# Attention features and a gated FFN on one core: Strassen products from batch 2 on, six PSUM banks for attention, omega by another queue

## The chip, the cores and the metric

The kernel runs on one core of a Trainium2 chip. The metric is the device time of one execution in microseconds. The time before is the median of three runs; the profile comes from one further execution of the same program.

## The reference

Linear attention with positive random features, then a feed-forward block with a gate. Sizes: batch B = 8, heads H = 8, sequence S = 576, head dimension D = 64, 128 features, model width 512, inner width 2048.

```python
def phi(x):                                   # x = q or k, scaled by 1 / D**0.25
    proj = einsum('bhsd,md->bhsm', x, omega)
    sq = sum(x * x, axis=-1, keepdims=True) / 2
    h = proj - sq
    h = h - max(h, axis=-1, keepdims=True)
    return exp(h) / sqrt(m)
...
kv  = einsum('bhsm,bhsd->bhmd', k_p, v)
z   = sum(k_p, axis=2)
num = einsum('bhsm,bhmd->bhsd', q_p, kv)
den = einsum('bhsm,bhm->bhs', q_p, z)[..., None] + 1e-06
x = (num / den).transpose(0, 2, 1, 3).reshape(B * S, H * D)
...
h = x @ w_in
sp = log1p(exp(h))
out = (h * erf(sp)) @ w_out
```

## The kernel before, in words

**The two halves of the work.** Attention is done by pairs of heads, 32 pairs in all, four to a batch. The pairs of batch 0 go one by one (`first`, `project_pair`); all later ones go in *quads* of two pairs (`attention`, `project`), of which each pair holds the keys or queries of two heads. For a quad, `project` multiplies keys or queries by omega in three groups of six matmuls of 128x128. Each of them uses only half of the rows of TensorE's array (64 of 128): pair j of the quad lies in the rows of its half, and its factor is `wq` for j = 0 and `wk` for j = 1 (both hold omega, in opposite halves). Each group fills two PSUM banks, one per pair (tiles `ppk_...` for keys and `ppq_...` for queries), and is followed by a maximum on VectorE, a shift, and an exponential on ScalarE, after which the two banks are free. `key_values`, `turn` and `attend` follow: keys times values (`kvp`), the queries' features turned (`pt`), numerator and denominator (`nd`), division into `xs`. `split` turns `xs` into a rounded half `xh` and a remainder `xl`.

The feed-forward block takes one batch at a time, in two *phases* ph = 0, 1 of 1024 inner columns each. A phase has four *granules* fp of the first product (256 columns each) and four blocks et of the second product. `BLOCKS` interleaves the granules of one phase with the second products of the phase before it. The operands of every product are held as a rounded part and a remainder, so a product takes three matmuls of 128x288: high by high, remainder by high, high by remainder. The one exception is the last product of attention, `nd`, for the pairs below `WHOLE` (8): these use whole F32 operands, and so have no remainders `ql` and `kl`.

**The first product in blocks.** A granule is a 2x2 block product. In the batches below `PLAIN` (3) `plain1` does it with eight block products, 48 matmuls (tiles `h...`). From batch `PLAIN` on `gemm1` does it with seven (the table `PRODUCTS`), 42 matmuls: their operands are sums of weight blocks (`S1` to `S4`) and of x blocks (`T1` to `T4`), and eight outputs are drained from PSUM, seven of them with an addition on VectorE (`hadd`, rows `hs<-hS,hs`) where `plain1` drains four with a copy (`hout`).

**The weights.** A weight unit (128 x 512) is made once from the 64-bit numbers in which it comes (`make`): a load `st`, a scaling copy `wt` on POOL (GpSimd) or ScalarE, three integer instructions on VectorE in a PSUM buffer `pw`, a rounded copy and a remainder `w`. It is then stored to DRAM (`wdw`) and fetched again for every later batch (`w<-wdw`). `make_sums` makes the sums S1 to S4 in batch PLAIN - 1, from two units of each granule: the two units are put together again (`R`, two instructions), four differences and sums (`S`), then rounded part and remainder (`cS`) in two units, both stored. `R` takes its buffer from the stream of `wt` and `S` from that of `st`, each of two buffers (`CAPS`).

**What sets the order.** `Plan` records all operations with their reads and writes. `Plan.order` plays the program through with costs for each operation (`COST` and the numbers at each `pl.op`), due times that follow from `plan=` and from successors, pools with a number of buffers (`SLOTS`), and streams with a cap on how many buffers are in use at a time (`CAPS`; `att` is the number of PSUM banks that attention may hold, 5 of 8, beside `moe1`, `moe2` and `pw`). Of the operations that an engine could start it takes the one that is due first. Going from full to half rows on TensorE or back costs half of `COST["turnout"]`, and after a projection the planner looks for another projection that is ready within `NEAR`. The result is one list, and every engine runs its instructions in exactly that order (`InOrder`); SyncE issues nearly all transfers, also in that order. So a change of one number can move instructions anywhere.

All instructions are recorded by one helper, so they all have the same line in the profile (L842) and are told apart by tile names. `ph`, `fp`, `et`, batch and pair numbers are in the names; the profile's groups leave them out.

**The start.** Omega comes by two transfers of POOL's queue into `om`; VectorE scales it and copies it to `wk` and `wq`. The keys and queries of pair 0 come by SyncE's queue in three parts each.

Of the kernel before, what the change touches and what calls it, by code (L numbers as in the profile page):

```python
# [10 lines left out]
F32 = mybir.dt.float32  # L11
F32R = mybir.dt.float32r
I32 = mybir.dt.int32
AF = mybir.ActivationFunctionType
ALU = mybir.AluOpType
# [40 lines left out]
            ("S4", "B22", (((0, 1), (0, 1)),)))  # L56


COST = dict(mm=0.132, proj=0.224, turnout=0.33, tr=0.109, kv=0.222, table=1.3)
LAG = {"T": 0.35, "A": 0.35, "V": 0.33, "G": 0.33, "S": 0.3}  # L60
SLOTS = dict(w=8, u=2, un=2, f=2, mx=2, sq=2, v=2, qh=1, ql=1, kh=1, kl=1, rc=2, xs=4, xh=2, xl=2, u2=2,
             hs=4, gs=2, gh=6, gl=6, os=4, ps=8)
CAPS = dict(st=2, wt=2, cv=2, att=5, moe1=3, moe2=2)

# [253 lines left out]
AHEAD = 40.0  # L318

BLOCKS = (("f", 0), ("f", 1), ("e", 0), ("f", 2), ("e", 1), ("f", 3), ("e", 2), ("e", 3))  # L320
WHOLE = 8
PLAIN = 3
PAIR = 6.9
FIRST = 11.5
LEAD = 30.0
# [13 lines left out]
RESTS0 = 15.0  # L339
SQA = 4.0  # L340
NEAR = 6.0
WHG = 5.0
WBG = -1e9


def build(emit):
# [190 lines left out]
    def project(m, qk, t0):  # L537
        a = quads[m]
        u, sq = a["u" + qk], a["sq" + qk]
        for j, x in enumerate(a["pairs"]):  # L540
            x["f" + qk] = pl.tile("f", f"f{qk}{x['nm']}", [P, NC, P])
        mx = pl.tile("mx", f"mx{qk}{a['nm']}", [P, 2, NC])
        for i in range(3):
            pps = [pl.tile("ps", f"pp{qk}{x['nm']}_{i}", [P, 512], F32, "att")
                   for x in a["pairs"]]
            pl.op("proj" + qk, [("T", 3 * COST["proj"], -1e9)],
                  lambda e, i=i, pps=pps: E.project(pps, u, i),
                  reads=[(u, 0)], writes=[(pp, 0) for pp in pps] + [(x["f" + qk], "room") for x in a["pairs"]], plan=quad_time(m, t0 + 0.02 * i))
            for j, pp in enumerate(pps):
                pl.op("max" + qk, [("V", 0.47, -1e9)], lambda e, i=i, j=j, pp=pp: E.maximum(sq.ap[:, j, :, 2], pp, i),  # L550
                      reads=[(pp, 0)], writes=[(sq, (j, (2, i)))])
            pl.op("shift" + qk, [("V", 0.17, -1e9)], lambda e, i=i: E.shift(mx, sq, i),
                  reads=[(sq, (j, x)) for j in range(2) for x in (0, 1, (2, i))],
                  writes=[(mx, (i, j)) for j in range(2)])
            for j, (x, pp) in enumerate(zip(a["pairs"], pps)):
                f = x["f" + qk]
                pl.op("exp" + qk, [("A", 0.77, -1e9)],
                      lambda e, i=i, j=j, f=f, pp=pp: E.exponential(f, mx, pp, i, j),
                      reads=[(pp, 0), (mx, (i, j))], writes=[(f, i)], set="exp")

    def key_values(n, t0):
        a = pairs[n]
        f, v = a["fk"], a["v"]
        kvp = a["kvp"] = pl.tile("ps", "kvp" + a["nm"], [P, 512], F32, "att", early(n))
        for j in range(2):
            pl.op("kv", [("T", (5 - j) * COST["kv"], -1e9)], lambda e, j=j: E.key_values(kvp, f, v, j),
                  reads=[(f, i) for i in range(3)] + [(v, 0)], writes=[(kvp, 0)],
                  plan=when(n, t0 + 0.08 * j))
        whole = n < WHOLE
        kh = a["kh"] = pl.tile("kh", "kh" + a["nm"], [P, 2, P], F32 if whole else F32R)  # L570
        kl = a["kl"] = kh if whole else pl.tile("kl", "kl" + a["nm"], [P, 2, P], F32R)
        pl.op("kvhigh", [("V", 0.4, -1e9), ("A", 0.4, -1e9)], lambda e: E.kv_high(e, kh, kvp),
              reads=[(kvp, 0)], writes=[(kh, 0)])
        if not whole:
            pl.op("kvrest", [("V", 0.4, -1e9)], lambda e: E.kv_rest(kl, kvp, kh),
                  reads=[(kvp, 0), (kh, 0)], writes=[(kl, 0)])

    def turn(n, t0):
# [246 lines left out]
def tile_attention_moe(ctx: ExitStack, tc: tile.TileContext, qT, kT, qN, kN, vP, omT, w1, w2, out):  # L825
# [66 lines left out]
    class Emit:  # L892
# [92 lines left out]
        def project(self, pps, u, i):  # L985
            for c in range(3):
                for j, pp in enumerate(pps):
                    r = slice(j * D, (j + 1) * D)
                    pe.matmul(pp.ap[:, c * P:(c + 1) * P],
                              lhsT=u.ap[r, (3 * i + c) * P:(3 * i + c + 1) * P], rhs=(wk if j else wq)[r],  # L990
                              start=True, stop=True)

        def maximum(self, m, pp, i):
            dve.tensor_reduce(m[:, 3 * i:3 * i + 3],
                              pp.ap[:, :3 * P].rearrange("p (c m) -> p c m", c=3), axis=AX.X,
                              op=ALU.max, negate=True)

        def shift(self, mx, sq, i):
            dve.tensor_reduce(mx.ap[:, :, 3 * i:3 * i + 3], sq.ap[:, :, 3 * i:3 * i + 3], axis=AX.X, op=ALU.add)

        def exponential(self, f, mx, pp, i, j):
            m = mx.ap if j is None else mx.ap[:, j]
            for c in range(3):
                act.activation(f.ap[:, 3 * i + c, :], pp.ap[:, c * P:(c + 1) * P], AF.Exp,
                               bias=m[:, 3 * i + c:3 * i + c + 1])
# [177 lines left out]
```

## Time and profile before

| what | us |
|---|---|
| median of three runs (lowest, highest) | 1059.65 (1059.07, 1060.84) |
| profiled execution | 1060.85 |
| span of the profiled execution | 1058.4 |
| mean granted clock of TensorE | 0.998 |

The span runs from the first to the last instruction that the trace records; the profiled execution's own time is 2.45 us longer than its span. An engine's busy time is the sum of what its instructions took, or less where they overlap. In a row of groups the operation stands with its output, an arrow, its inputs, their shapes and the count; behind the bar its busy time, the mean of one in ns, and the idle time of the engine before such instructions with what ended most of it. The view of waits has a waiting group, what it waited for, and then the total in us, the count and the mean. The timeline has the start, the duration and the row. A window has, for each engine, its busy time and in brackets the number of instructions.

The start of each half batch can be read from the first instruction of its first product: batch 0 starts at 36.7 us and its second half at 92.1, batch 1 at 159.6 and 239.0, batch 2 at 305.6 and 372.1, batch 3 at 439.0 and 501.9. The last second product ends at about 1054.8.

### The profile page before, as it was taken

How to read it: one execution, taken by the hardware profiler on the slowest of the kernel's cores; microseconds unless marked ns; L12 is line 12 of the kernel's file. 1: busy time of each engine (PE TensorE's matmuls, PEld its weight loads, DVE VectorE, ACT ScalarE, POOL GpSimd, SP SyncE). 2: the span in 40 equal slices, each digit the busy share in tenths (PEclk: the TensorE clock that was granted, in tenths of full speed). 3: DMA queues.
4: the chain of work that ended last, by engine and by line, in shares of the span. 5: the costliest groups of instructions: out<-in, count | busy, mean ns of one | idle time of the engine just before them, and what ended most of it. 6: DMA issues, size and time to landing. Idle time of an engine off the chain costs nothing.

```text
span 1058.4 us, 21952 instructions
## 1 busy us (share of the span) xinstructions
PE 1042.0 (98%) x8272; PEld 1014.2 (96%) x8272; DVE 752.0 (71%) x1488; ACT 681.9 (64%) x1302; POOL 458.8 (43%) x458
## 2 busy tenths in 40 slices
PE   7999999999999999999999999999999999999998
PEld 7889989999999999999999999999999999999998
DVE  5999997885587586765878766686677756765551
ACT  7879977776577766866647666485666656453330
POOL 6637446434297584632345243452326211443300
PEclk9999999999999999999999999999999999999999
DMA  8675878686366686668767677677866756668761
GB/s 256 207 269 184 281 260 280 232 297 227 130 226 227 250 289 239 218 209 296 251 236 233 234 257 243 220 249 261 259 203 227 235 181 226 222 231 265 269 234 49
DMA packets 77736, 247.81 MB, mean 234 GB/s; under 512 B 8736, under 2 KB 9120, under 8 KB 77632
## 3 DMA queue, kind: packets, MB, share of 16 engines
q1 hardware_dynamic: 77568, 246.35, 68.9%
q8 instruction: 66, 1.08, 0.4%
q14 instruction: 38, 0.31, 0.1%
q0 software_dynamic: 64, 0.07, 0.0%
HBM read 211.78 MB, written 34.60 MB: 233 GB/s over the span
## 4 chain that ended last, share of the span: by engine, by line
PE 92%; DVE 3%; DMA 2%; POOL 1%; issue 1%; SPq 1%; ACT 0%; DVEq 0%; POOLq 0%; ACTq 0%
PE o L842 39%; PE h L842 14%; PE hS L842 12%; PE hA L842 9%; PE kvp L842 5%; PE nd L842 4%; PE ppq L842 3%; PE ppk L842 3%; PE pt L842 2%; DMA uq<-qT 1%; DVE pw L842 1%; SPq L842 1%; POOL unq L842 0%; POOL uq L842 0%; POOL unk L842 0%
## 5 line engine op out<-in xcount | busy, mean ns | idle before, releaser
L842 PE MATMUL o<-gh,w 128*128 128x288 f32 x2048 | 458.7, 301 | 2.8 <-DVE w L842 2.5
L842 PEld LDWEIGHTS o<-gh,w 128*128 128x128 f32 x2048 | 341.5, 188 | 11.4 <-DVE w L842 3.0
L842 PE MATMUL o<-gl,w 128*128 128x288 f32 x1024 | 301.7, 295 | 0.0
L842 PEld LDWEIGHTS o<-gl,w 128*128 128x128 f32 x1024 | 192.9, 188 | 0.2
L842 PE MATMUL h<-xh,w 128*128 128x288 f32 x768 | 173.9, 303 | 0.3 <-ACT xh L842 0.3
L842 POOL TENSOR_TENSOR hs<-gs,hs 128x576 f32<-128x576 f32 x64 | 96.5, 1532 | 163.3 <-ACT gs L842 132.6
L842 PE MATMUL hS<-xh,wS 128*128 128x288 f32 x640 | 156.3, 297 | 0.1
L842 PEld LDWEIGHTS h<-xh,w 128*128 128x128 f32 x768 | 129.6, 190 | 1.9 <-ACT xh L842 0.5
L842 POOL TENSOR_TENSOR gl<-hs,gh 128x576 fp32r<-128x576 f32 x60 | 100.0, 1690 | 61.2 <-ACT gh L842 30.9
L842 PE MATMUL hA<-xh,w 128*128 128x288 f32 x480 | 122.1, 298 | 0.4 <-DVE u L842 0.4
L842 ACT ACT_TABLE_LOAD x92 | 118.0, 1283 | 2.4 <-PEq L1174 0.7
L842 PE MATMUL h<-xl,w 128*128 128x288 f32 x384 | 114.1, 297 | 0.5 <-POOL xl L842 0.5
L842 POOL TENSOR_TENSOR unq<-unq 128x288 f32<-128x288 f32 (+2 forms) x62 | 47.0, 759 | 153.0 <-ACT unq L842 146.5
L842 PEld LDWEIGHTS hS<-xh,wS 128*128 128x128 f32 x640 | 112.1, 188 | 0.3 <-DVE u L842 0.3
L842 ACT ACTIVATE fk<-ppk,mxk 128x128 f32<-128x128 f32 x288 | 79.2, 386 | 39.2 <-DVE mxk L842 35.1
L842 PE MATMUL hS<-xl,wS 128*128 128x288 f32 x320 | 94.3, 295 | 0.0
L842 ACT ACTIVATE rc<-nd,eps 64x288 f32<-64x288 f32 x128 | 63.5, 496 | 42.3 <-PE nd L842 40.0
L842 ACT ACTIVATE fq<-ppq,mxq 128x128 f32<-128x128 f32 x288 | 78.9, 386 | 16.6 <-DVE mxq L842 12.5
L842 ACT ACTIVATE gs<-hs 128x1152 f32<-128x1152 f32 x64 | 72.9, 1163 | 22.3 <-DVE hs L842 21.9
L842 PEld LDWEIGHTS hA<-xh,w 128*128 128x128 f32 x480 | 85.6, 188 | 0.6 <-DVE u L842 0.6
L842 POOL TENSOR_TENSOR unk<-unk 128x288 f32<-128x288 f32 (+2 forms) x72 | 58.5, 816 | 55.0 <-ACT unk L842 27.3
L842 PEld LDWEIGHTS h<-xl,w 128*128 128x128 f32 x384 | 73.0, 190 | 1.1 <-POOL xl L842 0.7
(111 smaller groups left out, 2127.1 us busy)
## 6 DMA issues: line engine op xcount, KB each, us to landing
w<-wdw SPq DMA_DIRECT2D x184, 512.0 KB, 4.5
wS<-wdcS SPq DMA_DIRECT2D x80, 512.0 KB, 4.3
st<-w SPq DMA_DIRECT2D x32, 512.0 KB, 4.4
wdw<-w SPq DMA_DIRECT2D x32, 512.0 KB, 3.9
v<-vP SPq DMA_DIRECT2D x32, 325.0 KB, 4.1
w<-wdw SPq DMA_DIRECT2D x40, 256.0 KB, 3.9
out<-os SPq DMA_DIRECT2D x32, 288.0 KB, 4.0
wdcS<-cS SPq DMA_DIRECT2D x16, 512.0 KB, 5.1
```

The costliest lines, as they stand in the source:

```text
L842: return tc.keep_in_program_order(method(*args, **kwargs))
```

## The change

There are four edits.

1. `PLAIN` goes from 3 to 2: batch 2 uses seven block products in place of eight, and the weights' sums are made in batch 1 in place of batch 2. `WHOLE` goes from 8 to 12: the attention of batch 2 uses whole F32 operands in `nd`.
2. `R` and `S` get a stream of their own (`sr`, `ss`), one buffer each, out of the same pools.
3. Attention may hold six PSUM banks; the planner's cost of a change of rows goes from 0.33 to 0.40. `project` and what follows it are written for any division of the nine chunks into groups (`GROUPS`); the table given has the same three groups of three, and `f` is now tracked by chunk.
4. Omega comes by two transfers of SyncE's queue, ahead of the first keys, directly to `wk` and `wq`, and is scaled there by two instructions; `om` and the two copies are gone.

```diff
-COST = dict(mm=0.132, proj=0.224, turnout=0.33, tr=0.109, kv=0.222, table=1.3)
+COST = dict(mm=0.132, proj=0.224, turnout=0.40, tr=0.109, kv=0.222, table=1.3)
...
-CAPS = dict(st=2, wt=2, cv=2, att=5, moe1=3, moe2=2)
+CAPS = dict(st=2, wt=2, cv=2, att=6, moe1=3, moe2=2)
...
-WHOLE = 8
-PLAIN = 3
+WHOLE = 12
+PLAIN = 2
...
+GROUPS = ((0, 3), (3, 6), (6, 9))
...
-        r = pl.tile("gh", f"R{ph}_{fp}", [P, 2, 2, BW], F32, "wt")
+        r = pl.tile("gh", f"R{ph}_{fp}", [P, 2, 2, BW], F32, "sr", 1)
...
-        s = pl.tile("gl", f"S{ph}_{fp}", [P, 4, BW], F32, "st")
+        s = pl.tile("gl", f"S{ph}_{fp}", [P, 4, BW], F32, "ss", 1)
...
-    om = sb.tile([P, P], F32, name="om", tag="os0")
-    pool.dma_start(om[D:P], omT)
-    pool.dma_start(om[0:D], omT)
+    sp.dma_start(wk[D:P], omT)
+    sp.dma_start(wq[0:D], omT)
...
-    dve.tensor_scalar_mul(om, om, 1.0 / math.sqrt(math.sqrt(D)))
-    dve.tensor_copy(wk[D:P], om[D:P])
-    dve.tensor_copy(wq[0:D], om[0:D])
+    for w in (wk[D:P], wq[0:D]):
+        dve.tensor_scalar_mul(w, w, 1.0 / math.sqrt(math.sqrt(D)))
```

Three places show how the order moves. The first is **TensorE's** order at the keys' projections of the second quad of batch 5. `ppk_2` and `ppk_3` are the banks of its two pairs, `uk` its keys, `o` a second product with gates `gh`, `gl` and a weight unit `w`. The last number of a name is a running one. Before:

```order
L842 MATMUL ppk_2_0_7844<-wq,uk_7081 128x128
L842 MATMUL ppk_3_0_7845<-wk,uk_7081 128x128
L842 MATMUL ppk_2_0_7844<-wq,uk_7081 128x128
L842 MATMUL ppk_3_0_7845<-wk,uk_7081 128x128
L842 MATMUL ppk_2_0_7844<-wq,uk_7081 128x128
L842 MATMUL ppk_3_0_7845<-wk,uk_7081 128x128
L842 MATMUL o_1_1_1_7857<-gh_1_0_6931,w_1_1_0_151_7631 128x288
L842 MATMUL o_1_1_1_7857<-gl_1_0_6955,w_1_1_0_151_7631 128x288
L842 MATMUL o_1_1_1_7857<-gh_1_0_6931,w_1_1_0_151_7631 128x288
L842 MATMUL o_1_1_0_7785<-gh_1_1_6949,w_1_1_0_151_7631 128x288
```

After:

```order
L858 MATMUL ppk_3_0_7866<-wk,uk_7076 128x128
L858 MATMUL ppk_2_3_7877<-wq,uk_7076 128x128
L858 MATMUL ppk_3_3_7878<-wk,uk_7076 128x128
L858 MATMUL ppk_2_3_7877<-wq,uk_7076 128x128
L858 MATMUL ppk_3_3_7878<-wk,uk_7076 128x128
L858 MATMUL ppk_2_3_7877<-wq,uk_7076 128x128
L858 MATMUL ppk_3_3_7878<-wk,uk_7076 128x128
L858 MATMUL ppk_2_6_7886<-wq,uk_7076 128x128
L858 MATMUL ppk_3_6_7887<-wk,uk_7076 128x128
L858 MATMUL ppk_2_6_7886<-wq,uk_7076 128x128
L858 MATMUL ppk_3_6_7887<-wk,uk_7076 128x128
L858 MATMUL ppk_2_6_7886<-wq,uk_7076 128x128
```

Before, one group of six stands alone between pieces of the second product, and 27 matmuls of the second product follow before the next group. After the change the three groups of the quad stand next to each other.

The second place is **VectorE's** order in the second half of batch 0, where the unit `w_0_2_1` of the second weight is made (three numbers: half, block, part). `pw_0_2_1` is the PSUM buffer in which it is put together, `xl` a remainder of x, `sqk` and `mxk` belong to the maxima of a quad's keys. The last row shown is the last step of the unit. Before:

```order
L842 TENSOR_TENSOR w_0_2_0_21_1880<-pw_0_2_0_1993,w_0_2_0_21_1880 128x2x256
L842 TENSOR_REDUCE mxk_1944<-sqk_1522 128x2x3 x2
L842 TENSOR_SCALAR pw_0_2_1_2052<-wt_0_2_1_2018 128x512
L842 SCALAR_TENSOR_TENSOR pw_0_2_1_2052<-st_0_2_1_1963,pw_0_2_1_2052 128x512 x2
L842 TENSOR_TENSOR xl_0_2054<-xs_2_1806,xh_0_2035 128x576
L842 TENSOR_TENSOR xl_1_2072<-xs_3_1900,xh_1_2040 128x576
L842 TENSOR_TENSOR w_0_2_1_22_1964<-pw_0_2_1_2052,w_0_2_1_22_1964 128x2x256
```

After:

```order
L858 TENSOR_REDUCE mxk_2008<-sqk_1519 128x2x3 x2
L858 TENSOR_SCALAR pw_0_2_1_2024<-wt_0_2_1_1978 128x512
L858 SCALAR_TENSOR_TENSOR pw_0_2_1_2024<-st_0_2_1_1926,pw_0_2_1_2024 128x512
L858 TENSOR_REDUCE sqk_1519<-ppk_0_6_2014 128x3
L858 TENSOR_REDUCE sqk_1519<-ppk_1_6_2015 128x3
L858 TENSOR_REDUCE mxk_2008<-sqk_1519 128x2x3
L858 SCALAR_TENSOR_TENSOR pw_0_2_1_2024<-st_0_2_1_1926,pw_0_2_1_2024 128x512
L858 TENSOR_TENSOR xl_1_2066<-xs_1_1247,xh_1_2029 128x576
L858 CAST w_0_2_1_22_1927<-pw_0_2_1_2024 128x2x256
L858 TENSOR_TENSOR w_0_2_1_22_1927<-pw_0_2_1_2024,w_0_2_1_22_1927 128x2x256
```

The unit's last step is row 250 of VectorE before and row 246 after. TensorE's first matmul with this unit is row 691 of its own before and row 700 after.

The third place is **POOL's** order in the first half of batch 1. `unk` and `unq` are squares of keys and queries of a later batch, `wt_1_1_1` and `wt_1_1_0` the scaling copies of units of the second weight's second half, `R`, `S` and `cS` belong to the weights' sums, `hs` is a gate. Before:

```order
L842 TENSOR_TENSOR unk_0_2496<-unk_0_2496 128x576
L842 TENSOR_TENSOR unk_0_2496<-unk_0_2496 128x9x32
L842 TENSOR_TENSOR unk_0_2496<-unk_0_2496 128x9x16
L842 TENSOR_SCALAR unk_0_2496<-unk_0_2496 128x9x16
L842 TENSOR_TENSOR unk_1_2514<-unk_1_2514 128x576
L842 TENSOR_TENSOR unk_1_2514<-unk_1_2514 128x9x32
L842 TENSOR_TENSOR unk_1_2514<-unk_1_2514 128x9x16
L842 TENSOR_SCALAR unk_1_2514<-unk_1_2514 128x9x16
L842 TENSOR_SCALAR wt_1_1_1_2640<-st_1_1_1_2539 128x512
L842 TENSOR_TENSOR hs_0_0_2351<-gs_0_0_2557,hs_0_0_2351 128x576 x2
```

After:

```order
L858 TENSOR_TENSOR S_1_2455<-R_1_2384,S_1_2455 128x256
L858 TENSOR_TENSOR cS_1_0_2510<-S_1_2455,cS_1_0_2510 128x2x256
L858 TENSOR_SCALAR cS_1_1_2550<-S_1_2455 128x2x256
L858 TENSOR_TENSOR R_2_2561<-w_0_4_31_2386 128x512
L858 TENSOR_TENSOR R_2_2561<-w_0_5_32_2432 128x512
L858 TENSOR_SCALAR wt_1_1_0_2611<-st_1_1_0_2543 128x512
L858 TENSOR_TENSOR unq_2_2153<-unq_2_2153 128x9x32
L858 TENSOR_TENSOR unq_2_2153<-unq_2_2153 128x9x16
```

Before, the copy `wt_1_1_1` stands behind the folds of two keys' squares. After the change the copy `wt_1_1_0` stands behind instructions of the sums: the last difference of the second granule's `S`, its `cS`, and both `R` of the third granule, which read units fetched from DRAM. In both programs two of the eight copies of that half are on POOL (`wt_1_1_1` and `wt_1_3_0` before, `wt_1_1_0` and `wt_1_3_0` after); the others are on ScalarE.

More of the change, by code (lines that the diff above doesn't have):

```diff
@@ L508, in project_pair @@
                   plan=pair_time(n, t0 + 0.05 * i))
-            pl.op("max" + qk, [("V", 0.47, -1e9)], lambda e, i=i, pp=pp: E.maximum(mx.ap, pp, i),
+            pl.op("max" + qk, [("V", 0.47, -1e9)], lambda e, i=i, pp=pp: E.maximum(mx.ap[:, 3 * i:3 * i + 3], pp.ap[:, :3 * P]),
                   reads=[(pp, 0)], writes=[(mx, i)])
-            pl.op("exp" + qk, [("A", 0.77, -1e9)], lambda e, i=i, pp=pp: E.exponential(f, mx, pp, i, None),
-                  reads=[(pp, 0), (mx, i)], writes=[(f, i)], set="exp")
+            pl.op("exp" + qk, [("A", 0.77, -1e9)], lambda e, i=i, pp=pp: E.exponential(
+                [(f, 3 * i + c, mx.ap[:, 3 * i + c:3 * i + c + 1], pp, c) for c in range(3)]),
+                  reads=[(pp, 0), (mx, i)], writes=[(f, 3 * i + c) for c in range(3)], set="exp")
     def load(m, qk):
@@ L542, in project @@
         mx = pl.tile("mx", f"mx{qk}{a['nm']}", [P, 2, NC])
[L543 to L559, printed above, removed]
@@ new lines, in project @@
+        fs = [x["f" + qk] for x in a["pairs"]]
+        for i, (first_, end) in enumerate(GROUPS):
+            pps, parts, place = [], [], {}
+            for c in range(first_, end, 4):
+                w = min(4, end - c)
+                both = False
+                for j in range(1 if both else 2):
+                    pp = pl.tile("ps", f"pp{qk}{a['pairs'][j]['nm']}_{c}", [P, 512], F32, "att")
+                    pps.append(pp)
+                    js = (0, 1) if both else (j,)
+                    chunks = [(x, c + k) for x in js for k in range(w)]
+                    place.update({x: (pp, k) for k, x in enumerate(chunks)})
+                    parts.append((pp, js, c, w, chunks))
+            pl.op("proj" + qk, [("T", (end - first_) * COST["proj"], -1e9)],
+                  lambda e, place=place: E.project(place, u),
+                  reads=[(u, 0)], writes=[(pp, 0) for pp in pps] + [(f, "room") for f in fs],
+                  plan=quad_time(m, t0 + 0.02 * i))
+            for k, (pp, js, c, w, chunks) in enumerate(parts):
+                n = len(chunks)
+                pl.op("max" + qk, [("V", 0.07 + 0.133 * n, -1e9)],
+                      lambda e, pp=pp, js=js, c=c, w=w, n=n: E.maximum(
+                          sq.ap[:, js[0]:js[-1] + 1, c:c + w, 2], pp.ap[:, :n * P]),
+                      reads=[(pp, 0)], writes=[(sq, (2, i, k))])
+            pl.op("shift" + qk, [("V", 0.17, -1e9)], lambda e, a=first_, b=end: E.shift(mx, sq, a, b),
+                  reads=[(sq, (j, x)) for j in range(2) for x in (0, 1)]
+                  + [(sq, (2, i, k)) for k in range(len(parts))], writes=[(mx, i)])
+            for pp, _, _, _, chunks in parts:
+                pl.op("exp" + qk, [("A", 0.02 + 0.25 * len(chunks), -1e9)],
+                      lambda e, pp=pp, chunks=chunks, place=place: E.exponential(
+                          [(fs[j], c, mx.ap[:, j, c:c + 1], pp, place[j, c][1]) for j, c in chunks]),
+                      reads=[(pp, 0), (mx, i)], writes=[(fs[j], c) for j, c in chunks], set="exp")
@@ L566, in key_values @@
             pl.op("kv", [("T", (5 - j) * COST["kv"], -1e9)], lambda e, j=j: E.key_values(kvp, f, v, j),
-                  reads=[(f, i) for i in range(3)] + [(v, 0)], writes=[(kvp, 0)],
+                  reads=[(f, c) for c in range(NC)] + [(v, 0)], writes=[(kvp, 0)],
                   plan=when(n, t0 + 0.08 * j))
@@ L586, in turn @@
             pl.op("turn", [("T", 3 * COST["tr"], -1e9)], lambda e, i=i, pt=pt: E.turn(pt, a["fq"], i),
-                  reads=[(a["fq"], i)], writes=[(pt, 0)], plan=when(n, t0 + 0.05 * i))
+                  reads=[(a["fq"], 3 * i + c) for c in range(3)], writes=[(pt, 0)], plan=when(n, t0 + 0.05 * i))
             pl.op("turnhigh", [("A", 0.39, -1e9), ("V", 0.47, -1e9)],
@@ L983, in sum_squares, with project, maximum, shift @@
                               axis=AX.X, op=ALU.add, negate=bool(x))
[L985 to L1005, printed above, removed]
+        def project(self, place, u):
+            for (j, c), (pp, k) in sorted(place.items(), key=lambda x: (x[0][1], x[0][0])):
+                r = slice(j * D, (j + 1) * D)
+                pe.matmul(pp.ap[:, k * P:(k + 1) * P], lhsT=u.ap[r, c * P:(c + 1) * P],
+                          rhs=(wk if j else wq)[r], start=True, stop=True)
+        def maximum(self, m, src):
+            dve.tensor_reduce(m, src.rearrange("p (j c m) -> p j c m", m=P, j=m.shape[1]) if len(m.shape) > 2
+                              else src.rearrange("p (c m) -> p c m", m=P), axis=AX.X, op=ALU.max,
+                              negate=True)
+        def shift(self, mx, sq, a, b):
+            dve.tensor_reduce(mx.ap[:, :, a:b], sq.ap[:, :, a:b], axis=AX.X, op=ALU.add)
+        def exponential(self, parts):
+            for f, c, m, pp, k in parts:
+                act.activation(f.ap[:, c, :], pp.ap[:, k * P:(k + 1) * P], AF.Exp, bias=m)
         def key_values(self, kvp, f, v, j):
```

## The prediction

> **What bounds the kernel now.** I read the page first: the shares of busy time and the chain.
>
> ```profile
> span 1058.4 us, 21952 instructions
> PE 1042.0 (98%) x8272; PEld 1014.2 (96%) x8272; DVE 752.0 (71%) x1488; ACT 681.9 (64%) x1302; POOL 458.8 (43%) x458
> ...
> PE 92%; DVE 3%; DMA 2%; POOL 1%; issue 1%; SPq 1%; ACT 0%; DVEq 0%; POOLq 0%; ACTq 0%
> ```
>
> TensorE (PE) is busy in 98% of the span and makes 92% of the chain, so what PE no longer has to issue shortens the run. VectorE (DVE) has 71%, but an average hides a stage in which it is full, and a 98% share says nothing of how the remaining 16 us are spread, so next I asked for the stages. By the first product of each batch, 100:172 is the end of batch 0 and the start of batch 1, 172:237 and 237:302 are batch 1, 302:372 and 372:437 are batch 2, 437:500 is the first half of batch 3.
>
> ```profile
> 100.00:172.00 72.00, 69.36 (x560) 64.98 (x560) 66.18 (x127) 60.36 (x134) 37.35 (x44) 1.00 0.80 269
> 172.00:237.00 65.00, 65.00 (x528) 63.16 (x526) 54.57 (x106) 47.33 (x91) 27.91 (x27) 1.00 0.78 264
> 237.00:302.00 65.00, 65.00 (x521) 63.57 (x520) 37.48 (x74) 43.94 (x84) 29.01 (x28) 1.00 0.53 179
> 302.00:372.00 70.00, 70.00 (x567) 68.02 (x566) 49.61 (x87) 48.88 (x95) 51.58 (x49) 1.00 0.69 242
> 372.00:437.00 65.00, 65.00 (x524) 63.30 (x523) 46.27 (x83) 46.06 (x88) 45.14 (x41) 1.00 0.68 239
> 437.00:500.00 63.00, 63.00 (x513) 61.58 (x512) 41.46 (x93) 42.58 (x86) 20.52 (x23) 1.00 0.75 257
> ```
>
> The columns are length, then busy time of PE, its weight loads, DVE, ACT and POOL, then granted clock, DMA share, GB/s. PE loses 2.64 us in the first stage, where DVE works 66.18 of 72 us; from 172 on it loses nothing, even in 302:437, where DVE and POOL make the weights' sums. So there are two regimes: until about 160 us DVE paces PE, after that PE alone. The view of waits names what PE waited for:
>
> ```profile
> PE ppk L842 <- DVE wk L842: 5.0, 1, 5.0
> PE o L842 <- DVE w L842: 2.5, 2, 1.6
> PE nd L842 <- DVE qh L842: 1.9, 1, 1.9
> PE ppq L842 <- DVE xs L842: 1.1, 1, 1.1
> ```
>
> The 2.5 us are two units of the second weight that DVE finished late.
>
> **Step 1: 48 products fewer.** Batch 2 takes 7 instead of 8 block products per granule: 6 matmuls of 128x288 fewer in each of 8 granules. The last long piece of the chain gives the price of one.
>
> ```profile
> 1021.45 33.37 PE o L842 x252
> ```
>
> 33.37 / 252 = 0.1324 us, times 48 is **-6.4 us**. PE is the pacer there (302:437 is full), so all of it counts.
>
> **Step 2: attention of batch 2 with whole operands.** 16 `nd` products change from three split matmuls, 3 x 0.1324 = 0.397 us, to one F32 product. A row of batch 0 prices that: x8 are four products with two records each.
>
> ```profile
> 46.95 2.10 PE L842 MATMUL nd<-qh,kh 128*128 128x288 f32 x8
> ...
> 49.02 0.30 PE L842 MATMUL h<-xl,w 128*128 128x288 f32 x1
> ```
>
> From 46.95 to 49.02 lie these four and one ordinary matmul: (2.07 - 0.13) / 4 = 0.485 us. 16 x 0.088 = **+1.4 us**. DVE loses 12 `ql` and 8 `kl` instructions, which makes room in batch 1, where this attention runs.
>
> **Step 3: six PSUM banks.** The projections of a quad come in three groups of 6 matmuls on half the rows. A group of two banks can start only when two of attention's banks are free; with six banks, two or three groups can stand next to each other. Each switch between half and full rows costs time, seen by comparing one group alone with two together:
>
> ```profile
> 145.16 0.29 PE L842 MATMUL h<-xh,w 128*128 128x288 f32 x1
> ...
> 146.25 0.40 PE L842 MATMUL h<-xh,w 128*128 128x288 f32 x1
> ...
> 491.03 0.29 PE L842 MATMUL o<-gh,w 128*128 128x288 f32 x1
> ...
> 492.80 0.40 PE L842 MATMUL o<-gh,w 128*128 128x288 f32 x1
> ```
>
> Between the starts of the neighbours lie 1.09 us for one group and 1.77 us for two; less one ordinary matmul that is 0.96 and 1.64, so a switch saved is worth 2 x 0.96 - 1.64 = 0.28 us. In the order of the program the 84 groups stand in 71 stretches before (58 single, 13 double) and in 57 after (34 single, 19 double, 4 triple): 14 x 0.28 = **-3.9 us**. Batches 0 and 1's first halves even get 4 more, so 18 go from where PE is the pacer (-5.0) and 4 come where it waits for DVE anyway (0 to +1.1).
>
> **Step 4: the two late units.** The place in DVE's order shown above ends the second late unit's preparation after 246 rows instead of 250, and PE's first use of it moves from row 691 to 700. By the page's means (752.0 / 1488 = 0.51 us on DVE, 1042.0 / 8272 = 0.13 on PE) that is 2.0 + 1.2 = 3.2 us earlier against its need, more than either wait. I take the 2.5 us as gone: **-2.5 us**, bounds 0 and the 2.64 of the stage. Next late would be the second-weight units of batch 1's first half (step 6).
>
> **Step 5: omega by SyncE's queue.**
>
> ```profile
> 0.75 1.84 SPq L842 DMA_DIRECT2D uk<-kT  x3
> 1.27 1.23 POOL L842 DMA_DIRECT2D om<-omT  x2 [0.82 <-POOLq L1174]
> 3.15 0.52 ACT L842 ACTIVATE uk<-uk 64x384 f32<-64x384 f32 x1 [1.12 <-DMA uk<-kT]
> 4.38 0.23 DVE L842 TENSOR_SCALAR om<-om 128x128 f32<-128x128 f32 x1 [3.12 <-DMA om<-omT]
> 4.97 4.18 PE L842 MATMUL ppk<-wk,uk 128*128 128x128 f32 x18 [4.97 <-DVE wk L842]
> ```
>
> Omega now lands before the keys. But SP needs 1.84 / 3 = 0.61 us per issue, and two issues now stand ahead of every load: the first key part is squared at about 3.15 + 1.2 = 4.4 instead of 3.15 us and is ready at 4.9, where PE started anyway. So the 5.0 us do not shrink; the key takes omega's place. All later loads of the start come up to 1.2 us later, against that POOL loses two issues, and one square of a key leaves ACT ahead of the `qh` copies that PE waited 1.9 us for. I take **0**, bounds -3.0 (both short waits gone) and +1.2.
>
> **Step 6: what the sums meet in batch 1.** These rows are the view of groups, kept apart by shape:
>
> ```profile
> L842 DVE TENSOR_TENSOR R<-w 128x512 f32<-128x512 f32 x9 | 11.3, 1275 | 2.7 <-DMA w<-wdw 2.7
> L842 POOL TENSOR_TENSOR R<-w 128x512 f32<-128x512 f32 x7 | 9.0, 1289 | 3.9 <-DMA w<-wdw 3.8
> L842 DVE TENSOR_TENSOR S<-R 128x256 f32<-128x256 f32 x8 | 7.5, 939 | 2.0 <-POOL R L842 2.0
> L842 DVE TENSOR_TENSOR cS<-S,cS 128x512 fp32r<-128x512 f32 x7 | 8.3, 1212 | 2.3 <-ACT cS L842 2.2
> L842 POOL TENSOR_TENSOR cS<-S,cS 128x512 fp32r<-128x512 f32 x9 | 14.3, 1607 | 1.9 <-ACT cS L842 1.7
> L842 DVE TENSOR_TENSOR w<-pw,w 128x512 fp32r<-128x512 f32 x32 | 22.0, 688 | 1.6 <-ACT w L842 1.0
> L842 DVE TENSOR_TENSOR hs<-hS,hs 128x288 f32<-128x288 f32 x80 | 36.2, 453 | 23.6 <-PE hS L842 23.0
> ```
>
> On DVE the sums are at least 11.3 + 7.5 + 8.3 = 27.1 us, on POOL 23.3 and more. They leave batch 2 and enter batch 1. In 237:302 there is room (DVE 37.48 of 65). In 172:237 DVE has 65 - 54.57 = 10.4 us left and also makes the second weight's units; half of the sums is 13.6 us, less what POOL takes over (27.91 of 65 there) and less the `ql` and `kl` that go. It fits, barely. In batch 2 the room they leave takes the 56 additions of the block products, 56 x 0.453 = 25.4 us of DVE, for 24 copies fewer; batch 3 of before is the same kind of work and lost nothing in 437:500. The transfers must fit too: 172:237 moves 65 us x 264 GB/s = 17.2 MB at a share of 0.78; the stores of eight sums add 8 x 0.524 = 4.2 MB, by proportion a share of 0.97, and what slides finds room in 237:302 (0.53). I put step 6 at **+1.2 us**, bounds 0 (as in 302:437, where the same sums cost PE nothing) and +5.3 (twice the 2.64 of the stage that DVE paced).
>
> The row w<-pw,w reads one of its inputs from PSUM and takes 688 ns; R<-w has both in SBUF and takes 1275 for as many elements. The Trainium skill, "SBUF — State Buffer", section "Who interferes with whom", says that a DVE instruction with two SBUF inputs contends with GpSimd's reads, one with a single SBUF input not. The rows agree. By it the preparation of the second weight keeps its speed next to sums on POOL, and only DVE's gates and remainders in batch 1 get slower; taking them all as dear as R, 0.59 us more for each of the 4 there in 172:237, would be 2.4 us of DVE, which still fits into 10.4.
>
> **The sum.** -6.4 + 1.4 - 3.9 - 2.5 + 0 + 1.2 = -10.2 us. The profiled execution took 1060.85 us (span 1058.4 and 2.45 around it), 1.2 above the median of 1059.65; -10.2 gives 1050.65 on the one and 1049.45 on the other. I forecast the median, **1049.4 us**.
>
> **Rivals.** *Batch 1 gives it back* (0.24): the units of the second weight come late in 172:237 as they came in 100:172, and the rest of step 6's bound is paid: 4 us over the forecast, 1053 to 1056. For it: DVE's 10.4 us are used up and the DMA share comes to 0.97. Against: 302:437, and weights are fetched ahead of their use. *More than the sum* (0.11): the start. After PE's short waits the granted clock fell:
>
> ```profile
> 56.00:58.00 2.00, 2.00 (x17) 1.88 (x15) 1.97 (x5) 1.61 (x6) 0.00 (x0) 0.72 0.17 16
> 58.00:60.00 2.00, 2.00 (x10) 2.00 (x10) 1.97 (x7) 1.18 (x5) 0.00 (x0) 0.50 0.86 328
> ```
>
> At 0.50 for some 3.4 us (0.28 x 2 / 0.5 = 1.1 in the first row, all of the second, a little after) PE loses 1.7 us. If the waits before it shrink, this and step 5's 3.0 go: down to 1049.4 - 4.7, so 1044.7 to 1046.5. The Trainium skill, "TensorE: Matmul & The Clock Gate", Part 1, gives a window of 3.4 us and half speed after an idle one; the row agrees in both, and by it a wait that only shortens PE's work in that window can cost as much again. *Slower* (0.05): POOL's queue in batch 1. The place in POOL's order shown above puts the bias copy of a second-weight unit behind R, S and cS of a sum, which wait for two fetched units. Behind that copy wait DVE's preparation and PE's second product. Eight units, each late by the 1.6 us of the longest such wait, are 12.8 us: 1049.4 + 12.8 = 1062.2. It decides from 1.6 us on for all eight, or 10.2 in sum; against it, only two of the eight copies are on POOL. *The switches are worth nothing* (0.05), because the time of a group is hidden elsewhere: 1053.3; joined groups also ask for ACT and DVE in a burst.
>
> **How the numbers follow.** The forecast's own range, 1046.5 to 1053, has 0.55. The range is from the low rival's lower part to the upper end of the give-back, 1045 to 1056, and leaves out the slower rival and the tails. Within 0.2% (about what a measurement of this kernel can tell from no change) is 1057.5 to 1061.8: only a give-back beyond its bound, 0.05 of its 0.24. Slower 0.05, faster 0.90.
>
> **What would show it.** Step 1: 48 h matmuls fewer, PE full in 302:437. Step 2: 96 F32 records of `nd`. Step 3: PE's time between o and h pieces around joined groups, 0.28 us per join. Step 4: no wait of o for DVE w near 155 us. Step 5: PE starts at 4.9 us, now behind uk. Step 6: PE at 65.00 of 65 in batch 1. Wrong would be: a wait of o for w in batch 1 above 3 us, or PE idle when batch 2's first products ask for sums that are not stored yet.

## The result, and the profile after

| | median us | runs (lowest to highest) |
|---|---|---|
| before, with the runs beside the changed kernel | 1059.36 | 4 (1058.50 to 1060.84) |
| changed | 1048.74 | 4 (1047.39 to 1049.21) |
| ratio | 0.9896 | 95% interval 0.9879 to 0.9913 |

The kernel became 10.6 us faster; forecast were 10.2. The profiled execution took 1049.21 us, 11.6 less than that of before. The page of the changed kernel, its first rows and the head of the chain:

```profile
span 1047.3 us, 21906 instructions
PE 1033.3 (99%) x8208; PEld 1006.1 (96%) x8208; DVE 757.0 (72%) x1521; ACT 678.3 (65%) x1282; POOL 466.9 (45%) x469
...
PE 93%; DVE 2%; POOL 1%; DMA 1%; ACT 1%; SPq 1%; issue 1%; DVEq 0%; ACTq 0%
```

PE has 64 records fewer: 48 of `h`, and 16 of `nd`, where 16 F32 products with two records each replace 48 single ones. The stages of the changed kernel, in the same columns as before, and its waits:

```profile
100.00:172.00 72.00, 71.46 (x581) 67.49 (x580) 69.45 (x127) 58.47 (x131) 41.04 (x44) 1.00 0.79 278
172.00:237.00 65.00, 64.98 (x508) 62.72 (x507) 59.37 (x102) 49.72 (x95) 53.57 (x54) 1.00 0.86 307
237.00:302.00 65.00, 65.00 (x514) 62.67 (x513) 49.87 (x85) 47.47 (x93) 47.00 (x46) 1.00 0.77 257
302.00:372.00 70.00, 69.83 (x570) 68.16 (x569) 49.81 (x111) 45.67 (x91) 25.33 (x27) 1.00 0.73 258
```

```profile
PE ppk L858 <- ACT uk L858: 5.1, 1, 5.1
PE o L858 <- DMA w<-wdw: 1.4, 1, 1.4
PE ppk L858 <- DVE xs L858: 0.9, 2, 0.7
PE ppk L858 <- ACT fk L858: 0.8, 2, 0.5
PE o L858 <- ACT fk L858: 0.5, 1, 0.5
```

The waits of `o` for a unit that DVE finished late are gone, the start now waits for the key. The 1.4 us for a unit fetched from DRAM lie at 927 us, in batch 7, where the kernel before waits 0.3. In batch 1, where the sums now stand, PE loses 0.02 us: in its first half DVE rose from 54.57 to 59.37 of 65 us, POOL from 27.91 to 53.57, and the DMA share from 0.78 to 0.86. Where the time went shows in the first products of batches 2 and 3, of before and then of the changed kernel (there also of the second half of batch 6, for use below):

```profile
305.56 0.30 PE L842 MATMUL h<-xh,w 128*128 128x288 f32 x1
...
438.99 0.29 PE L842 MATMUL hA<-xh,w 128*128 128x288 f32 x1
```

```profile
306.53 0.30 PE L858 MATMUL hA<-xh,w 128*128 128x288 f32 x1
...
431.95 0.29 PE L858 MATMUL hA<-xh,w 128*128 128x288 f32 x1
...
868.10 0.29 PE L858 MATMUL hA<-xh,w 128*128 128x288 f32 x1
```

Up to batch 2 the changed kernel gains nothing (1.0 us later). Batch 2 takes 125.42 instead of 133.43 us: 8.0 of the gain. The remaining 4.1 come from there to the end, where 24 stretches of projections stand instead of 34 (a stretch is a row of half-row groups on PE with no full-row matmul between them).

### The profile page after: what moved, and what is told of

Its sections match the earlier page's. It is cut to its first block, busy times and chain, and to the rows that moved or that the text cites. A ratio compares the mean times of both kernels' runs of the same rounds, so it can differ in the third digit from the quotient of the medians.

```text
span 1047.3 us, 21906 instructions
## 1 busy us (share of the span) xinstructions
PE 1033.3 (99%) x8208; PEld 1006.1 (96%) x8208; DVE 757.0 (72%) x1521; ACT 678.3 (65%) x1282; POOL 466.9 (45%) x469
## 4 chain that ended last, share of the span: by engine, by line
PE 93%; DVE 2%; POOL 1%; DMA 1%; ACT 1%; SPq 1%; issue 1%; DVEq 0%; ACTq 0%
PE o L858 39%; PE hS L858 15%; PE hA L858 11%; PE h L858 9%; PE kvp L858 6%; PE nd L858 5%; PE ppq L858 3%; PE ppk L858 3%; PE pt L858 3%; DVE pw L858 1%; SPq L858 1%; DMA uq<-qT 1%; POOL unk L858 1%; ACT rc L858 0%; DVE xs L858 0%
## 5 line engine op out<-in xcount | busy, mean ns | idle before, releaser
L858 PE MATMUL hS<-xh,wS 128*128 128x288 f32 x768 | 186.4, 298 | 0.2 <-ACT hs L858 0.2
L858 PE MATMUL hA<-xh,w 128*128 128x288 f32 x576 | 148.3, 298 | 0.0
L858 PEld LDWEIGHTS hS<-xh,wS 128*128 128x128 f32 x768 | 134.3, 188 | 0.4 <-ACT hs L858 0.4
L858 PE MATMUL h<-xh,w 128*128 128x288 f32 x512 | 119.5, 309 | 0.0
L858 PE MATMUL hS<-xl,wS 128*128 128x288 f32 x384 | 113.3, 295 | 0.0
L858 PEld LDWEIGHTS hA<-xh,w 128*128 128x128 f32 x576 | 103.3, 188 | 0.0
L858 PEld LDWEIGHTS h<-xh,w 128*128 128x128 f32 x512 | 86.5, 190 | 2.7 <-DVE os L858 0.3
L858 PE MATMUL hA<-xl,w 128*128 128x288 f32 x288 | 85.1, 296 | 0.0
L858 PE MATMUL h<-xl,w 128*128 128x288 f32 x256 | 76.1, 297 | 0.4 <-POOL xl L858 0.3
L858 PEld LDWEIGHTS hS<-xl,wS 128*128 128x128 f32 x384 | 72.4, 188 | 0.0
```

Source lines behind the costliest of these rows:

```text
L858: return tc.keep_in_program_order(method(*args, **kwargs))
```

## The experiments

Every ratio is to the kernel before on the same chip, over five rounds.

| run | median us | ratio, 95% interval |
|---|---|---|
| e9 streams alone | 1060.56 | 0.9993, 0.9981 to 1.0006 |
| e10 banks alone | 1054.62 | 0.9941, 0.9923 to 0.9960 |
| e5 products alone | 1064.13 | 1.0027, 1.0015 to 1.0039 |
| e1 changed, five banks | 1056.72 | 0.9962, 0.9949 to 0.9975 |
| e2 changed, batch 2 plain | 1054.86 | 0.9954, 0.9940 to 0.9968 |
| e8 changed, buffers shared | 1064.86 | 1.0035, 1.0013 to 1.0056 |
| e4 changed, omega by POOL | 1048.09 | 0.9879, 0.9864 to 0.9895 |
| e12 changed again | 1048.80 | 0.9889, 0.9869 to 0.9908 |
| e3 changed, groups apart | 1056.55 | 0.9961, 0.9947 to 0.9976 |
| e6 changed, WHOLE 8 | 1049.44 | 0.9891, 0.9878 to 0.9904 |
| e7 changed, idle filled | 1051.12 | 0.9907, 0.9895 to 0.9920 |
| e11 another order | 1046.08 | 0.9857, 0.9837 to 0.9877 |

One of e9's twelve runs took 2041 us, which nothing here explains; it is not in the ratio.

### What a switch of rows costs

**e3** keeps the planned list and only moves the last of joined projection groups behind the next operation of PE:

```diff
         self.busy, self.span = busy, max(o.end for o in ops)
+        i = 0
+        while i < len(out):
+            o = out[i]
+            i += 1
+            if o == "table" or not o.half:
+                continue
+            ts = [(k, x) for k, x in enumerate(out[i:i + 60], i) if x != "table" and x.eng == "T"][:2]
+            if len(ts) == 2 and ts[0][1].half and not ts[1][1].half:
+                (a, p), (b, _) = ts
+                if not any(x in p.succ for x in out[a:b + 1] if x != "table"):
+                    out.insert(b, out.pop(a))
...
         return out
```

> The changed kernel with its order as planned, except that in 22 places the last of the projection groups that stand next to each other is put behind the next operation of TensorE: 79 stretches instead of 57, 50 instead of 32 from batch 2 on. No instruction comes or goes. Theory (0.28 us per switch): 18 x 0.28 = 5.0 us longer, with 0 to 1.1 more for the four in batches 0 and 1: 1053.7 to 1054.9. Rival (a switch is hidden, or the price is that of VectorE's and ScalarE's work on the groups): 1048.7, within 0.5.

Measured: 0.0065 above the changed kernel's ratio, 6.9 us. The first products of batch 2 and of the second half of batch 6 in e3:

```profile
305.42 0.30 PE L870 MATMUL hA<-xh,w 128*128 128x288 f32 x1
...
874.08 0.29 PE L870 MATMUL hA<-xh,w 128*128 128x288 f32 x1
```

Between them lie 568.66 us, in the changed kernel 561.57: 7.09 us for 18 switches, **0.394 each**, not 0.28. The windows between these rows, of e3 and then of the changed kernel, show that nothing else changed there:

```profile
305.42:874.08 568.66, 568.49 (x4592) 553.99 (x4591) 398.57 (x873) 372.14 (x687) 222.83 (x222) 1.00 0.69 239
```

```profile
306.53:868.10 561.57, 561.40 (x4593) 552.05 (x4592) 398.68 (x874) 370.96 (x687) 222.77 (x222) 1.00 0.71 242
```

PE is idle for 0.17 us in both, and VectorE has the same work, so the 7.09 us are not waits for VectorE or ScalarE. The switch is real and its price was too small. The reason stands in the timeline of before, in the row behind the one at 146.25 that the prediction used as the neighbour of the single group:

```profile
146.49 0.30 PE L842 MATMUL h<-xl,w 128*128 128x288 f32 x1
```

The first full-row matmul after a stretch keeps PE for 0.24 us (146.25 to 146.49) instead of 0.13, and the prediction's measure ended at its start. With it a single group costs 1.07 and two together 1.74, and a switch saved is 0.40. The changed kernel's four stretches of three groups cost 2.40 each by the same measure, again 0.40 less per switch. From batch 2 on every single group of the kernel before costs 1.06 or 1.07, and all stretches together take 54.4 us there (46 of them) and 48.9 in the changed kernel (32), with no wait in any. The Trainium skill, "TensorEngine Tiling (Array Packing)", section "Key Properties", says that changing the tiling mode, unlike changing the tile, drains the engine; the rows agree and give the price.

**e1** sets `att` to 5 and `turnout` to 0.33 in the changed kernel; **e10** sets them to 6 and 0.40 in the kernel before, and nothing else. The diff is e1's:

```diff
-COST = dict(mm=0.132, proj=0.224, turnout=0.40, tr=0.109, kv=0.222, table=1.3)
+COST = dict(mm=0.132, proj=0.224, turnout=0.33, tr=0.109, kv=0.222, table=1.3)
...
-CAPS = dict(st=2, wt=2, cv=2, att=6, moe1=3, moe2=2)
+CAPS = dict(st=2, wt=2, cv=2, att=5, moe1=3, moe2=2)
```

> The changed kernel with five PSUM banks for attention and the planner's cost of a switch back at 0.33; the rest as changed. In its order the 84 projection groups stand in 68 stretches instead of 57, from batch 2 on in 43 instead of 32. Theory (each switch saved is worth 0.28 us of TensorE): 11 x 0.28 = 3.1 us longer than the changed kernel, so about 1051.8 beside its 1048.7, and the time between the neighbours of a stretch stays 0.96 for one group, 1.63 for two. Rival (the switches hide behind other work): within 0.5 us of the changed kernel.

> The kernel before with six PSUM banks for attention and the planner's cost of 0.40, nothing else. Theory: 35 instead of 46 stretches from batch 2 on, 11 x 0.39 = 4.3 us; and the waits of o for DVE w near 155 us (2.5 in the kernel before) shrink to below 1: together 5.8 to 6.8 below the kernel before, a ratio near 0.994. Rival (the late units went for another reason, such as the moved sums): 4.3 below, 0.996, with 2.5 us of these waits left.

e1 was 7.0 us above the changed kernel (0.0066), more than its theory: 11 switches at 0.394 are 4.3, and the waits for late units came back, with waits for `qh` that the changed kernel doesn't have, as its view of waits shows:

```profile
PE o L858 <- DVE w L858: 2.5, 2, 1.6
PE nd L858 <- ACT qh L858: 2.4, 1, 2.4
PE nd L858 <- DVE qh L858: 1.1, 1, 1.1
```

These parts are more than 7.0 together; how far they overlap was not measured.

e10 was 6.2 us below the kernel before, within its theory (5.8 to 6.8), and its view of waits has no wait of `o` for DVE's `w`. From the first product of batch 2 to the last second product it takes 744.9 instead of 749.2 us, 4.4 for 11 switches. So the late units went because of the banks and the planner's cost, and step 4 needs no moved sums. Both runs change the two numbers together; which of them does it was not tried apart.

### The sums' buffers

**e5** makes only the change of products in the kernel before (`PLAIN = 2`, `WHOLE = 12`); **e2** undoes it in the changed kernel; **e8** puts only `R` and `S` back into the shared streams, in the changed kernel; **e9** only gives them their own, in the kernel before. The diff is e8's:

```diff
-        r = pl.tile("gh", f"R{ph}_{fp}", [P, 2, 2, BW], F32, "sr", 1)
+        r = pl.tile("gh", f"R{ph}_{fp}", [P, 2, 2, BW], F32, "wt")
...
-        s = pl.tile("gl", f"S{ph}_{fp}", [P, 4, BW], F32, "ss", 1)
+        s = pl.tile("gl", f"S{ph}_{fp}", [P, 4, BW], F32, "st")
```

> The changed kernel with batch 2 back at eight block products and attention of pairs 8 to 11 back in three matmuls (PLAIN 3, WHOLE 8). Theory: 48 products of 0.1324 us come back (+6.4), 16 whole products of 0.485 become three of 0.132 (-1.4), and four more stretches from batch 2 on (36 instead of 32) add 4 x 0.28 = 1.1: 6.1 longer, about 1054.8. Rival (the sums in batch 1 cost 4 us there, which come back): about 1050.8, with TensorE's waits between 172 and 302 us gone that the changed kernel would have to show.

> The kernel before with PLAIN 2 and WHOLE 12 alone: five banks, the sums' buffers shared, omega by POOL's queue. Theory, with the price of a stretch corrected to 0.39 us by the runs so far (the first matmul after a stretch also takes 0.24 instead of 0.13 us): 48 products fewer, -6.4; 16 whole products, +1.4; 41 instead of 46 stretches from batch 2 on, -2.0: 7.0 below the kernel before, a ratio of 0.9934, and from the first product of batch 2 on 8.4 shorter. Rival (sums in batch 1 give back when they share buffers with the second weight's units): 3 below, 0.997, with waits of o for w between 160 and 300 us.

> The changed kernel with R and S in the streams of wt and st again. The order from batch 2 on keeps 32 stretches; before it 23 instead of 25. Theory (buffers of their own matter little, because TensorE is the pacer where the sums are made): within 0.8 us of the changed kernel. Rival (the second weight's units wait for a buffer that a sum holds): 2 us or more longer, with waits of o for w between 170 and 240 us.

> The kernel before with the buffers of R and S in streams of their own, nothing else. Theory (the buffers decide only where the sums are made beside units of the second weight, which in the kernel before they are not): no change, within 0.8 us of the kernel before, the same 71 stretches. Rival (buffers of their own speed the kernel up by themselves): 2 us or more below.

e2: 0.0058 above the changed kernel, 6.1 us, as worked out (with the four switches at 0.394 it would be 6.6). e9: no change, as expected. e5 is 2.9 us **slower** than the kernel before, and e8 14.7 us slower than the changed kernel (1.0035 against 0.9896): the rival in both, at a far higher price than I gave it. Stages and waits of e8:

```profile
172.00:237.00 65.00, 59.28 (x440) 56.03 (x439) 49.70 (x89) 51.08 (x98) 40.91 (x43) 0.96 0.72 247
237.00:302.00 65.00, 62.64 (x467) 59.27 (x467) 48.66 (x79) 40.16 (x87) 32.39 (x30) 0.99 0.78 271
```

```profile
PE o L858 <- ACT w L858: 3.7, 2, 2.6
PE o L858 <- DVE w L858: 3.1, 6, 1.5
```

e5 has such waits too (3.7 us for ACT's `w`, and 4.4 for DVE's, of which the kernel before has 2.5). PE loses 8.1 us in e8's batch 1 while DVE and POOL have **less** work there than in the changed kernel (49.70 against 59.37 and 40.91 against 53.57 in its first half), and the DMA share of that half is lower. No engine is short; the units come late because they are started late. The eight loads of raw units in that half, of e8 and then of the changed kernel (count, issue times least/median/most in ns, first and last start):

```profile
L858 SPq DMA_DIRECT2D st<-w x8: 328/330/736, 176.8 to 248.6; - x8
```

```profile
L858 SPq DMA_DIRECT2D st<-w x8: 327/424/1003, 166.5 to 220.3; - x8
```

With `S` in the stream of `st` the loads spread over 71.8 us, with buffers of its own over 53.8. A sum holds one of the two buffers through `S` and `cS`, and the unit behind it may not even be loaded. Two of the eight loads of e8 start 0.02 to 0.03 us after a sum's last step on DVE, as a load does that waited for the sum's buffer:

```profile
207.49 0.73 DVE L858 TENSOR_TENSOR cS<-S,cS 128x512 fp32r<-128x512 f32 x1
208.25 0.33 SPq L858 DMA_DIRECT2D st<-w  x1
...
221.95 0.69 DVE L858 TENSOR_TENSOR cS<-S,cS 128x512 fp32r<-128x512 f32 x1
222.66 0.55 SPq L858 DMA_DIRECT2D st<-w  x1
```

The clock comes on top: it halves for 3.4 us after the wait of 1.5 us at 194 and again after the one of 2.6 at 231, 1.7 us of PE each time. Idle time and clock are 11.5 of the 13.6 us by which the first product of batch 2 is later in e8 (320.16 instead of 306.53); the rest stays open. `R` and `S` were put back together, so which stream costs more is open.

### Whole operands, omega, the clock

> The changed kernel with the attention of batch 2 in three matmuls again (WHOLE 8), nothing else. Theory (TensorE is the pacer in batch 1 too): 16 x (0.485 - 0.397) = 1.4 us shorter than the changed kernel. Rival (VectorE has no room in batch 1 for the twelve remainders of queries and eight of keys, and TensorE waits for units of the second weight): 1 to 4 us longer, with waits of o for w or nd for ql between 160 and 300 us.

e6 (`WHOLE = 8`) did not become faster: its ratio is 0.0005 below the changed kernel's, well inside the intervals. PE loses 1.86 us in the second half of batch 1, where the changed kernel loses nothing, and has new waits:

```profile
237.00:302.00 65.00, 63.14 (x502) 61.30 (x502) 50.40 (x82) 46.41 (x88) 46.85 (x46) 1.00 0.79 284
```

```profile
PE h L858 <- ACT hs L858: 1.0, 2, 0.5
PE h L858 <- DVE ql L858: 0.9, 1, 0.9
```

The time that whole operands cost on PE thus buys about as much: in this order PE would have waited for a remainder `ql` and for `hs`.

> The changed kernel with omega by POOL's queue and the copies on VectorE, as before; the planned order is the same. Theory (the key took omega's place): TensorE starts at 4.97 instead of 5.08 us, and the time is within 0.5 of the changed kernel's 1048.7. Rival 1 (two issues ahead of every load cost 1.2 us): 1047.5. Rival 2 (POOL's two issues hold up its squares): 1049.7 or more.

e4 starts PE at 4.81 instead of 5.08 us. Its ratio is 0.0010 to 0.0017 below those of the two measurements of the changed kernel, whose intervals overlap with its own: omega's new way gains nothing, and whether it loses a microsecond stays open. e4 has the planned order of the changed kernel, and so shows something else: what the clock costs. The same place in the changed kernel, then in e4:

```profile
57.52 0.58 PE L858 MATMUL ppk<-wk,uk 64*128 64x128 f32 x1 [0.29 <-ACT fk L858]
...
57.90 0.42 PE L858 MATMUL ppk<-wk,uk 64*128 64x128 f32 x1
...
63.19 0.39 PE L858 MATMUL kvp<-v,fk 128*128 128x130 f32 x2
```

```profile
57.67 0.37 PE L858 MATMUL ppk<-wk,uk 64*128 64x128 f32 x1 [0.29 <-ACT fk L858]
...
57.88 0.27 PE L858 MATMUL ppk<-wk,uk 64*128 64x128 f32 x1
...
61.81 0.27 PE L858 MATMUL kvp<-v,fk 128*128 128x130 f32 x1
```

Up to there both run alike; then the changed kernel's clock halves for 3.4 us and e4's does not: 1.38 + 0.15 = 1.5 us. Each run's mean clock tells whether that happened (1.000, 0.998 for one such stretch), and both occur for one kernel. Where it falls decides its price: in e10, whose order is the same there, it falls at 52.7 to 56.1 us, and e10 is 0.9 us ahead of e4 both before it and behind it. There it cost nothing, since PE in e4 waits in that place (0.28 us for `xl`, 0.47 for `fk`).

**e7** adds six matmuls without use ahead of the last projection group there:

```diff
+FILL = 6
...
         def project(self, place, u):
+            if u.name == "uk_2":
+                for _ in range(FILL if (0, 6) in place else 0):
+                    self.spare()
+                free = place[0, min(c for _, c in place)][0].ap[:, 3 * P:4 * P]
+                self.spare = lambda: pe.matmul(free, lhsT=u.ap[:D, :P], rhs=wq[:D],
+                                               start=True, stop=True)
```

> The changed kernel with six matmuls of 64x128 more, whose result nothing uses, ahead of the third projection group of batch 1's first keys, where TensorE waits some 0.6 us near 56 us. Theory (the half clock of 3.4 us that follows is set off by these waits, and costs 1.5 to 1.7 us): the granted clock is 1.0 at 56 to 64 us in all runs, and those runs are 1.0 to 1.7 us shorter than runs of the changed kernel with a mean clock of 0.998. Rival (the half clock comes by itself, or the fill is too short): the runs divide as before into 1.0 and 0.998, and the median does not move by more than 0.5.

A miss: the clock fell in all five runs (0.995 to 0.998), and the ratio is 0.0011 to 0.0018 above those of the changed kernel, with intervals that overlap. The fill waited itself, since it writes into a bank that ACT still reads, and in the profiled run the clock had fallen before it. The stretch 54:56 of e7, and in its timeline the row with the fill and the first projections behind it:

```profile
54.00:56.00 2.00, 2.00 (x11) 1.78 (x9) 2.00 (x7) 0.47 (x3) 1.07 (x2) 0.50 0.00 0
```

```profile
57.31 1.82 PE L859 MATMUL ppk<-wq,uk 64*128 64x128 f32 x14 [0.61 <-ACT fk L859]
```

Whether a fill at the right place holds the clock was not settled.

### Another order, and the changed kernel again

**e11** has `WHOLE = 8`, `NEAR = 12.0`, `START0 = 4 * FIRST + 3` and omega by POOL.

> The changed kernel with WHOLE 8, NEAR 12, START0 two us earlier and omega by POOL's queue: 32 stretches from batch 2 on as in the changed kernel, 23 instead of 25 before it. Theory (three matmuls per product are 1.4 us shorter where nothing waits for ql; the order decides that): 1 to 3 us below the changed kernel. Rival (the remainders of queries make TensorE wait in the second half of batch 1 as in the run with WHOLE 8 alone): 0 to 2 us above it.

> The changed kernel once more, on the same chip as the three others, so that they can be compared. Expected: a ratio of 0.988 to 0.991 to the kernel before. In runs with a mean granted clock of 1.0 a span 1.5 us shorter than in those with 0.998.

e11 is 2.7 us below the changed kernel on the same chip (1046.08 to 1048.80; its runs end at 1046.77, those of the changed kernel begin at 1047.93) and faster than both kernels. Its batch 1 is full again with three matmuls per product:

```profile
172.00:237.00 65.00, 65.00 (x527) 63.52 (x526) 59.58 (x107) 51.68 (x101) 52.86 (x53) 1.00 0.83 296
237.00:302.00 65.00, 65.00 (x528) 63.98 (x528) 55.79 (x93) 49.42 (x98) 54.25 (x49) 1.00 0.79 278
```

So in this order the choice that held PE up in e6 holds up nothing. Three numbers and omega's way were changed at once; which of them made the 2.7 us was not tried apart. About 0.9 of it is the wait for a unit from DRAM in batch 7, 0.3 us in e11 and 1.2 in e12.

## Why the prediction was right, step by step

- **Two regimes, PE the pacer from 160 us on**: right. 302:372 has PE at 69.83 of 70, and what PE no longer issues there shortened the run one for one.
- **Step 1 (-6.4)**: right. Batch 2 has 12 stretches of projections before and 8 after, so 48 x 0.1324 + 4 x 0.394 = 7.9, measured 8.0; e2 gave the whole part of the change back as 6.1.
- **Step 2 (+1.4)**: right as PE's price, a little high. From their start to the start of the second instruction behind them, less one ordinary matmul, the sixteen products take 0.415 us each in batch 1 of the kernel before and 0.483 in the changed kernel: +1.1. It was not a pure cost: e6 shows that the work which it takes from DVE would have cost PE about as much in batch 1.
- **Step 3 (-3.9)**: mechanism right, size too small. The term was mis-sized because the measure left out the matmul behind a stretch: 14 x 0.394 = -5.5, and the stretches of both traces give the same (54.4 to 48.9).
- **Step 4 (-2.5)**: right in effect (no wait of `o` for DVE's `w` is left); 0.5 us of a wait for ACT's `fk` stands in its place. e1 and e10 show the banks, with the planner's cost, as its cause.
- **Step 5 (0)**: right for the start: the key takes omega's place, 5.08 us where 4.9 was worked out. Its effect on the whole time lies within the noise of e4.
- **Step 6 (+1.2)**: the forecast's weak step. It asked whether DVE, POOL and the DMAs have room for the sums in batch 1, and they have (0.02 us lost there). It gave no term to the edit on which that depends: without buffers of their own the same sums cost 14.7 us in e8, and e5 came out 9.9 above its theory. *Batch 1 gives it back* is what happens without this edit, and the prediction did not see that; it took the rival's price from the engines' room, where a shared buffer decides. The *slower* rival's queue of POOL did not form: no wait of `o` for `w` in batch 1.
- **The sum**: -6.4 + 1.1 - 5.5 - 2.0 + 0 + 0 = -12.8 with the measured sizes, against 11.6 in the profiled execution and 10.6 between the medians. So about 1 to 2 us are lost where the prediction saw none, before batch 2: its first product starts 1.0 us later though PE's idle time there fell by 3.1. Two parts can be read. Three more matmuls of the second product stand ahead of that first product (576 instead of 573 records, 0.4 us). And the first projection groups of batch 1, at 50 to 59 us, take 0.7 us longer beside their named waits: 4.95 in e4 and 4.25 in e9, which has the order of the kernel before, both at a clock of 1.00. That they wait for banks inside is an inference; the rest of the loss stays open.
- **The number**: that it came within 0.4 us is partly luck. Step 3 was 1.6 us too small, and step 6 put down 1.2 that were not paid; the loss before batch 2 and the 0.5 of step 4 made up for them.
- **The start's clock** (*more than the sum*): the half clock stayed, in the changed kernel's runs mostly once. Its price, 1.7 us in the prediction, is 1.5 between the changed kernel and e4.

## What to carry to other kernels

Before moving work into a stage, look past the engines' idle time at the buffers that it would share there: sums that hold one of two buffers delayed the weights behind them and cost 14.7 us, more than twice what the saved matmuls are worth, with PE, DVE and POOL less busy in that batch. Measure the price of a switch to the start of the second instruction after it. And try parts of a change alone: here the buffers' streams were worth nothing by themselves (e9), the products were a loss by themselves (e5), and with both in place the products are worth 6.1 us (e2).

## What the runs showed of the hardware

- The granted clock can halve for 3.4 us after waits that are each short. These windows of the changed kernel lead up to it; the longest single wait in the 10 us before is the one of 0.7 us at 50 us (`ppk` for DVE's `xs` in the view of waits above):

```profile
54.00:56.00 2.00, 1.62 (x9) 1.18 (x9) 2.00 (x7) 0.48 (x2) 1.29 (x2) 1.00 0.00 0
56.00:58.00 2.00, 1.25 (x9) 0.82 (x9) 1.97 (x5) 2.00 (x9) 0.00 (x0) 0.88 0.37 147
58.00:60.00 2.00, 2.00 (x14) 1.78 (x13) 1.97 (x6) 1.01 (x4) 0.00 (x0) 0.50 0.96 305
```

  The Trainium skill, "TensorE: Matmul & The Clock Gate", Part 1, calls the window free-running and the outcome variable from run to run; the changed kernel and e4, alike in order up to here, agree. Its table of the two states names an idle window of some 3.4 us as what comes before the slow one; in these rows PE was busy for 1.62 and 1.25 of 2 us when the clock fell, so no whole idle window stood before it. The row that the prediction called in agreement shows half speed and the length, not an idle window.
- A DVE addition with both inputs in SBUF took 0.68 us twice in e8, once with POOL idle and once with POOL at work for half of it, and 0.98 to 1.9 in the changed kernel, each time beside POOL's additions for sums or gates. The rows are of e8 and of the changed kernel (durations least/median/most in ns):

```profile
L858 DVE TENSOR_TENSOR R<-w x2: 680/682/684, 194.6 to 218.0; 128x512 f32<-128x512 f32 x2
```

```profile
L858 DVE TENSOR_TENSOR R<-w x3: 982/1781/1905, 178.3 to 248.0; 128x512 f32<-128x512 f32 x3
```

  The unit's own step `w<-pw,w`, with one input in PSUM, kept 675 to 691 ns in the same stretch, beside POOL's `R` too. This is as the Trainium skill, "SBUF — State Buffer", section "Who interferes with whom", has it; the prediction weighed that rule.
